# Order of VectorE's query copy and of the two folds of the exponential sums in a cached attention kernel

## The chip, the cores and the metric

One core of a Trainium2 chip. The metric is the device time of one execution in microseconds (us). The engines are named as in the profile: TensorE (PE) for matmuls, VectorE (DVE), ScalarE (ACT), GpSimd (POOL), and the queues that issue DMAs, above all SP.

## The reference

`x` has 2048 tokens of 512 values; there are 32 heads of 128, with caches of 2048 keys and values each.

```python
xn = layernorm(A_x)
q  = (xn @ A_wq) per head                       # 32 heads of 128
p  = softmax(q @ k_cache.T * 128**-0.5)         # 2048 x 2048 per head
s  = concat(p @ v_cache) @ A_wo
h  = gelu(layernorm(xn) @ B_w1)                 # then shifted by 1, -1, 2, -2 tokens
x1 = xn + shifted(h) @ B_w2
g  = silu(x1 + gelu(layernorm(x1) @ B_w3) @ B_w4)
out = A_x + s * g
```

All tensors are bf16.

## The kernel before, in words

The attention is cut into 128 **units**: groups of four heads, within each the four blocks of 512 queries, within each block the four heads. Each unit has 8 **slots**. In slot `p` of unit `u` (one turn of the loop that ends the function) TensorE makes the scores of 2 x 128 keys against 512 queries (`s_slot`, line 187): two matmuls into one of two PSUM buffers `ps_s`. ScalarE exponentiates them into `pT` (line 198). The products with the values (`pv_slot`) run some slots behind, ten in the turned units (below), so that TensorE does not wait for the exponentials. A slot thus has four matmuls, and mostly two more:

- slots 0 and 1: the queries of unit `u + 2` (`q_mm`, line 171) into the PSUM tile `ps_q`;
- slots 4 and 5: the output projection of an older block (`wo_mm`, line 291) into `ps_wo`;
- slots 2, 3, 6 and 7: a piece of the MLP branch (`ps_m`), spread over the run by a table of chunks.

`ps_q` and `ps_wo` have the same tag `xa` in the pool `psX`, which has one buffer for each tag (line 105). So the projection of slot 4 cannot start before the queries of slots 0 and 1 have been copied out by `q_copy` (line 179, VectorE, the cast at L184), and the next queries not before VectorE has added `ps_wo` to its accumulator (`wo_post`, L353).

VectorE also sums the exponentials, for the softmax's denominators. `add_first` (L204, slot 4) adds the first two `pT` tiles of a unit into `acc` (128 x 4 x 512), `add_next` (L209) adds the third in slot 6, and the fourth in slot 0 of the next unit. Then come two **folds**, of four columns to two (L214) and of two to one (L215). The function `add_last` holds the fourth add and both folds.

What remains is a sum over partitions, which is done in two ways. Outside the units 32 to 113, four matmuls against ones do it (`sums`). In the units 32 to 113 (`turned`, line 241) a DMA turns the folded `acc`: `acc_turn` (L247, issued by SP in slot 3 of the next unit) writes `accT`, and `turned_sums` reduces it on VectorE (L252) in slot 0 of the unit after. In both ways the reciprocals go to DRAM and are broadcast from there into `rb` (`bcast`, SP, L269), and `norm` multiplies the attention's result with them (L279 in turned units).

The order is written out by hand: every instruction is pinned to the program's order on its engine or queue (`pin`), and an engine takes them strictly in that order, so an instruction that waits holds up those behind it. In a turned unit VectorE's order is: reduce and reciprocal of unit `u - 2`, the fourth add and the folds of `u - 1` (slot 0), the copy of the queries (slot 2), an MLP polynomial (L454) where one is due in slot 2, `add_first` (slot 4), `wo_post` and `add_next` (slot 6), MLP work that is due then, and `norm` (slot 7). On SP: the write of the reciprocals, the broadcast (slot 2), the turn (slot 3), and then loads of keys, values and weights, which are issued well ahead of their use.

Of the kernel before, what the change touches and what calls it, by code (L numbers as in the profile page):

```python
# [17 lines left out]
def kernel(  # L18
# [32 lines left out]
    HG = 4 if H % 4 == 0 else (2 if H % 2 == 0 else 1)  # L51
# [71 lines left out]
    NU = len(units)  # L123
# [10 lines left out]
    def at(n, fn):  # L134
        todo[n].append(fn)
# [35 lines left out]
    def q_mm(u, dcs):  # L171
        g, qt, hh = units[u]
        if dcs[0] == 0:
            st[u] = dict(psq=psX.tile([P, 512], FP32, tag="xm" if u == HG else "xa", name="ps_q"))
        for dc in dcs:
            mm(st[u]["psq"][:], wqs[g * HG + hh][:, dc, :],
               xnT[:, dc, qt * 512:(qt + 1) * 512], dc == 0, dc == DC - 1)

    def q_copy(u):
        qT = qtp.tile([P, 512], BF16, name="qT")  # L180
        if u > QUIET + 1:
            pin(nc.scalar.activation(out=qT[:], in_=st[u].pop("psq")[:], func=ACT.Identity))
        else:
            pin(nc.vector.tensor_copy(out=qT[:], in_=st[u].pop("psq")[:]))  # L184
        st[u]["qT"] = qT

    def s_slot(u, p):
        g, qt, hh = units[u]
        s = st[u]
        sps = psS.tile([P, 2, 512], FP32, name="ps_s")  # L190
        for j in range(2):
            kc = 2 * p + j
            kv = kTs[g * HG + hh].rearrange("d (i p j) -> d i j p", p=P, j=KJ)
            mm(sps[:, j, :], kv[:, kc // KJ, kc % KJ, :], s["qT"][:], True, True)
        if p % 2 == 0:
            s.setdefault("pT", []).append(ptp.tile([P, 4, 512], BF16, name="pT"))
        jj = 2 * (p % 2)
        pin(nc.scalar.activation(  # L198
            out=s["pT"][-1][:, jj:jj + 2, :], in_=sps[:], func=ACT.Exp, scale=SCALE))
# [7 lines left out]
    def add_next(u, i):  # L207
        a = st[u]["acc"]
        pin(nc.vector.tensor_tensor(out=a[:], in0=a[:], in1=st[u]["pT"][i][:], op=ALU.add))  # L209

    def add_last(u):
        add_next(u, 3)
        a = st[u]["acc"]
        pin(nc.vector.tensor_tensor(out=a[:, 0:2, :], in0=a[:, 0:2, :], in1=a[:, 2:4, :], op=ALU.add))  # L214
        pin(nc.vector.tensor_tensor(out=a[:, 0, :], in0=a[:, 0, :], in1=a[:, 1, :], op=ALU.add))  # L215

    def pv_slot(u, p):
        g, qt, hh = units[u]
        s = st[u]
        if p == 0:  # L220
            s["o"] = psO.tile([P, 512], FP32, name="ps_o")
        pT = s["pT"][p // 2]
        for j in range(2):
            kc = 2 * p + j
            mm(s["o"][:], vBs[g * HG + hh][:, kc, :], pT[:, 2 * (p % 2) + j, :], kc == 0, kc == KC - 1)

    def sums(u):
        s = st[u]
        ps = psX.tile([P, 4], FP32, tag="xa" if u + 1 < QUIET else "xm", name="ps_sum")
        a = s["acc"][:, 0, :].rearrange("k (p j) -> k j p", j=4)  # L230
        for j in range(4):
            mm(ps[:, j:j + 1], a[:, j, :], ones_t[:], True, True)
        recip(s, ps)
# [7 lines left out]
    def turned(u):  # L241
        return T0 <= u < T1

    def acc_turn(u):
        s = st[u]
        s["at"] = atp.tile([P, 4, P], BF16, name="accT")
        pin(nc.sync.dma_start_transpose(out=s["at"][:], in_=s["acc"][:, 0, :]))  # L247

    def turned_sums(u):
        s = st[u]  # L250
        sm = smp.tile([P, 4], FP32, name="sm")
        pin(nc.vector.tensor_reduce(  # L252
            out=sm[:], in_=s.pop("at")[:], axis=mybir.AxisListType.X, op=ALU.add))
        recip(s, sm)
# [12 lines left out]
    def bcast(u):  # L267
        st[u]["rb"] = rp.tile([P, 512], FP32, name="rb")
        pin(nc.sync.dma_start(  # L269
            out=st[u]["rb"][:], in_=st[u]["dr"][:].rearrange("a b -> (a b)").partition_broadcast(P)))  # L270
# [20 lines left out]
    def wo_mm(g, t, hhs):  # L291
        if hhs[0] == 0:
            wo_box[0] = psX.tile([P, D], FP32, tag="xa", name="ps_wo")
        held = g == NG - 1 and (NG - 2, t // 4) in deferred
        if held and hhs[0] == 0:
            wo_part(wo_box[0][:], g - 1, t, range(HG), True, False)
        wo_part(wo_box[0][:], g, t, hhs, hhs[0] == 0 and not held, hhs[-1] == HG - 1)
# [49 lines left out]
    def wo_post(g, t):  # L347
        ps = wo_box.pop(0)
        sa = s_acc[:, t, :]
        if g == 0:  # L350
            pin(nc.vector.tensor_copy(out=sa, in_=ps[:]))
            return
        pin(nc.vector.tensor_tensor(out=sa, in0=ps[:], in1=sa, op=ALU.add))  # L353

    def wo_out(t):
        sa = s_acc[:, t, :]
        xl, gl = fin.pop(t)
        pin(nc.vector.scalar_tensor_tensor(
            out=gl[:], in0=sa, scalar=0.5, in1=gl[:], op0=ALU.mult, op1=ALU.mult))
        pin(nc.vector.tensor_tensor(out=xl[:], in0=gl[:], in1=xl[:], op=ALU.add))  # L360
        pin(nc.sync.dma_start(out=out2d[t * P:(t + 1) * P, :], in_=xl[:]))
# [361 lines left out]
    def normed(u):  # L723
        norm(u)
        gg, qq, hh = units[u]
        if hh == HG - 1 and (gg, qq) in deferred:
            pin(nc.sync.dma_start(out=o_d[qq][:], in_=oTs[(gg, qq)][:]))
        elif hh == HG - 1:
            wo_todo.extend((gg, 4 * qq + ts) for ts in range(4))
            if gg == NG - 1:  # L730
                fin_load(4 * qq)

    for n in range(NS):
        u, p = divmod(n, SPU)
        s_slot(u, p)
        lag = next(v for lim, v in LAGS if n < lim)
        while pv_done <= n - lag:
            pv_slot(*divmod(pv_done, SPU))
            pv_done += 1
        if u == 0 and p in (1, 3, 5):  # L740
            q_mm(1 + p // 2, range(DC))
        if u == 0 and p in (2, 4, 6):
            q_copy(p // 2)
        if u == HG - 2 and p in (6, 7):
            q_mm(HG, (2 * p - 12, 2 * p - 11))
        if u == HG - 2 and p == 7:
            q_copy(HG)
        if p in (0, 1) and HG - 1 <= u < NU - 2:
            q_mm(u + 2, (2 * p, 2 * p + 1))
        if p == 0 and u >= 2 and turned(u - 2):  # L750
            turned_sums(u - 2)
        if p == 0 and u >= 1:
            add_last(u - 1)
        if p == 3 and u >= 1 and turned(u - 1):
            acc_turn(u - 1)
        if p == 2 and u >= 2 and turned(u - 2):
            bcast(u - 2)
        if p == 2 and HG - 1 <= u < NU - 2:
            q_copy(u + 2)
        if p == (4 if u == T1 + 2 else 2) and u >= 2 and not turned(u - 2):  # L760
            normed(u - 2)
        if p == 3 and u >= 1 and not turned(u - 1):
            sums(u - 1)
        if p == 4 and u >= 1 and u != T1 + 1 and not turned(u - 1):
            bcast(u - 1)
        if p in (4, 5) and wo_todo:
            wo_mm(*wo_todo[0], (0, 1) if p == 4 else (2, 3))
        if p == 6 and QUIET <= u < NU - 1:
            add_next(u, 2)
        if p == 6 and wo_box:  # L770
            gg, t = wo_todo.popleft()
            wo_post(gg, t)
            if gg == NG - 1:
                at(n + 5, lambda t=t: wo_out(t))
                if t % 4 < 3:
                    fin_load(t + 1)
        if p == 4:
            add_first(u)
        if p == 4 and u == NU - 1:
            a = st[u]["acc"]  # L780
            pin(nc.vector.tensor_tensor(out=a[:, 0:2, :], in0=a[:, 0:2, :], in1=a[:, 2:4, :], op=ALU.add))
        if p == 6 and u < QUIET:
            add_next(u, 2)
        if p in (2, 3, 6, 7):
            w = 2 * u + (p >= 4)
            i = p % 2
            if i == 0:
                want = -(-(w + 1 - W0) * NCH // (W1 - W0)) if w >= W0 else 0
                window.pop("run", None)
                if done < min(want, NCH):  # L790
                    if done in hooks:
                        hooks.pop(done)(n)
                    window["run"] = chunks.popleft()
                    done += 1
            if "run" in window:
                window["run"](i, n)
        for fn in todo.pop(n, ()):
            fn()
        if p == SPU - 1 and u >= 2 and turned(u - 2):
            normed(u - 2)  # L800
        if p == SPU - 1 and u == T1 + 1:
            bcast(T1)
# [78 lines left out]
```

## Time and profile before

| | |
|---|---|
| median of 3 runs | 1278.13 us (1277.34 to 1278.28) |
| profiled execution, its time | 1277.01 us |
| its span, first to last instruction | 1275.2 us |
| mean granted TensorE clock | 0.999 |
| TensorE matmul busy | 1259.0 us |
| VectorE busy | 1094.0 us |
| ScalarE busy | 1110.9 us |
| GpSimd busy | 142.2 us |

The span runs from the first to the last instruction of one profiled execution; its time is 1.8 us longer. Busy time is the time that an engine spends in instructions. A matmul's row lasts longer than the distance to the next matmul's start, because matmuls are pipelined. In lists of groups, the columns are the source line, the engine, the operation, what is written and read, the count, and then busy us, mean ns of one, and the idle time just before them with what ended it.

### The profile page before, as it was taken

The numbers are of one execution on the slowest core, as the hardware profiler recorded it, in microseconds if no ns is written. First come the engines' busy times: TensorE is split into PE (matmuls) and PEld (weight loads), VectorE is DVE, ScalarE is ACT, GpSimd is POOL, SyncE is SP. The second block draws the span as 40 slices with busy tenths as digits, with TensorE's granted clock in tenths as the row PEclk, the third lists the DMA queues.
The fourth block names the chain that finished last, engine by engine and source line by source line (L and its number), as shares of the span: only waits on it lengthen the run. The fifth ranks groups of instructions, "written<-read, shape, count | busy, mean of one in ns | idle before, by whom it ended". The sixth has DMA issues, their size and how long they took to land.

```text
span 1275.2 us, 16720 instructions
## 1 busy us (share of the span) xinstructions
PE 1259.0 (99%) x5992; PEld 601.6 (47%) x5992; DVE 1094.0 (86%) x1489; ACT 1110.9 (87%) x1195; POOL 142.2 (11%) x241
## 2 busy tenths in 40 slices
PE   8999999999999999999999999999999999999998
PEld 5444444444444444444444444444444444444444
DVE  7888879899888988889898888988888899887886
ACT  7899998888999988899988889998888999987883
POOL 4420003334110010000000000000000000000111
PEclk9999999999999999999999999999999999999999
DMA  9644243355544454344454354535546334551532
GB/s 183 135 93 69 52 80 98 95 120 120 129 93 87 108 121 95 60 93 96 96 100 95 75 91 96 104 73 93 100 95 114 65 71 88 107 126 42 141 74 68
DMA packets 217556, 122.51 MB, mean 96 GB/s; under 512 B 169408, under 2 KB 194496, under 8 KB 217472
## 3 DMA queue, kind: packets, MB, share of 16 engines
q1 hardware_dynamic: 208512, 96.26, 38.8%
q0 software_dynamic: 8672, 24.91, 7.8%
q8 instruction: 47, 0.77, 0.3%
q14 instruction: 37, 0.30, 0.1%
q10 hardware_dynamic: 288, 0.26, 0.1%
HBM read 82.58 MB, written 7.60 MB: 71 GB/s over the span
## 4 chain that ended last, share of the span: by engine, by line
PE 69%; DVE 14%; ACT 13%; DMA 2%; issue 1%; POOL 0%; DVEq 0%; SPq 0%; POOLq 0%
PE ps_s L115 25%; PE ps_o L115 24%; ACT pT L198 9%; PE ps_m L115 7%; PE ps_wo L115 6%; PE ps_q L115 6%; DVE acc L209 4%; DVE oT L279 1%; DVE acc L214 1%; ACT pre L480 1%; DVE qT L184 1%; DVE h2T L462 1%; ACT sq L459 1%; DVE sm L252 1%; ACT sq L450 1%
## 5 line engine op out<-in xcount | busy, mean ns | idle before, releaser
L198 ACT ACTIVATE pT<-ps_s 128x1024 bf16<-128x1024 f32 x1024 | 1012.8, 1033 | 139.9 <-PE ps_s L115 130.9
L115 PE MATMUL ps_s<-qT,kT 128*128 128x512 bf16 x2048 | 608.5, 379 | 2.4 <-ACT pT L198 0.8
L115 PE MATMUL ps_o<-pT,vb 128*128 128x512 bf16 x2048 | 607.7, 379 | 0.0
L115 PEld LDWEIGHTS <-kT 128*128 128x128 bf16 x2048 | 229.4, 113 | 233.8 <-issue 21.9
L209 DVE TENSOR_TENSOR acc<-acc,pT 128x2048 bf16<-128x2048 bf16 x254 | 307.7, 1211 | 24.9 <-ACT pT L198 22.7
L115 PEld LDWEIGHTS <-vb 128*128 128x128 bf16 x2048 | 199.6, 98 | 225.3
L204 DVE TENSOR_TENSOR acc<-pT 128x2048 bf16<-128x2048 bf16 x128 | 156.2, 1220 | 28.2 <-ACT pT L198 26.7
L115 PE MATMUL ps_q<-xnT,wq_h 128*128 128x512 bf16 (+1 forms) x524 | 151.8, 374 | 2.1 <-DMA xnT<-xn 1.5
L115 PE MATMUL ps_wo<-wo_h,oT 128*128 128x512 bf16 x468 | 138.8, 379 | 2.9 <-DVE qT L184 2.6
L353 DVE TENSOR_TENSOR s_acc<-ps_wo,s_acc 128x512 f32<-128x512 f32 x100 | 68.8, 688 | 57.4 <-PE ps_wo L115 57.3
L214 DVE TENSOR_TENSOR acc<-acc 128x1024 bf16<-128x1024 bf16 x127 | 87.9, 692 | 4.3
L279 DVE TENSOR_TENSOR oT<-ps_o,rb 128x512 bf16<-128x512 f32 x82 | 87.8, 1071 | 0.1
L184 DVE CAST qT<-ps_q 128x512 bf16<-128x512 f32 x122 | 83.4, 684 | 4.8 <-PE ps_q L115 4.8
L115 PEld LDWEIGHTS <-wq_h 128*128 128x128 bf16 x524 | 50.6, 98 | 62.7 <-issue 3.1
L115 PEld LDWEIGHTS <-oT 128*128 128x128 bf16 x480 | 46.9, 98 | 63.3 <-issue 9.8
L115 PE MATMUL ps_m<-xn2T,w_sb 128*128 128x512 bf16 x224 | 66.6, 379 | 0.0
L115 PE MATMUL ps_m<-w_sb,h2T 128*128 128x512 bf16 x224 | 64.0, 379 | 0.0
L603 POOL DMA_DIRECT2D w_sb<-in_B_w_dram x28 | 21.2, 757 | 365.5 <-PE ps_m L115 330.3
L215 DVE TENSOR_TENSOR acc<-acc 128x512 bf16<-128x512 bf16 x127 | 54.0, 425 | 4.3
L252 DVE TENSOR_REDUCE sm<-accT 128x4 f32<-128x512 bf16 x82 | 55.7, 679 | 1.0 <-DMA accT<-acc 1.0
L635 POOL DMA_DIRECT2D g_d<-xr x16 | 8.8, 549 | 319.4 <-DVE xr L633 319.4
L454 DVE SCALAR_TENSOR_TENSOR sq<-sq,pre 128x1024 bf16<-128x1024 bf16 x36 | 43.8, 1217 | 0.0
(77 smaller groups left out, 613.6 us busy)
## 6 DMA issues: line engine op xcount, KB each, us to landing
rb<-dr SPq DMA_DIRECT2D x128, 256.0 KB, 4.2
vb<-in_A_v_cache_dram SPq DMA_DIRECT2D x64, 256.0 KB, 4.1
w_sb<-in_B_w_dram POOLq DMA_DIRECT2D x28, 256.0 KB, 3.9
wo_h<-in_A_wo_dram SPq DMA_DIRECT2D x32, 128.0 KB, 3.7
wq_h<-in_A_wq_dram SPq DMA_DIRECT2D x28, 128.0 KB, 3.4
kT<-in_A_k_cache_dram SPq DMA_TRANSPOSE x128, 3.8
dr<-rc SPq DMA_DIRECT2D x128, 2.0 KB, 1.4
xr<-in_A_x_dram POOLq DMA_DIRECT2D x16, 128.0 KB, 3.3
```

The source lines that it names most:

```text
L115: pin(nc.tensor.matmul(out=out, lhsT=lhsT, rhs=rhs, start=start, stop=stop))
L184: pin(nc.vector.tensor_copy(out=qT[:], in_=st[u].pop("psq")[:]))
L198: pin(nc.scalar.activation(out=s["pT"][-1][:, jj:jj + 2, :], in_=sps[:], func=ACT.Exp, scale=SCALE))
L204: pin(nc.vector.tensor_tensor(out=s["acc"][:], in0=s["pT"][0][:], in1=s["pT"][1][:], op=ALU.add))
L209: pin(nc.vector.tensor_tensor(out=a[:], in0=a[:], in1=st[u]["pT"][i][:], op=ALU.add))
L214: pin(nc.vector.tensor_tensor(out=a[:, 0:2, :], in0=a[:, 0:2, :], in1=a[:, 2:4, :], op=ALU.add))
L215: pin(nc.vector.tensor_tensor(out=a[:, 0, :], in0=a[:, 0, :], in1=a[:, 1, :], op=ALU.add))
L252: pin(nc.vector.tensor_reduce(out=sm[:], in_=s.pop("at")[:], axis=mybir.AxisListType.X, op=ALU.add))
L279: pin(nc.vector.tensor_tensor(out=oTs[(g, qt)][:, hh, :].rearrange(f, j=4), in0=s["o"].rearrange(f, j=4), in1=s["rb"].rearrange("x (p j) - ...
L353: pin(nc.vector.tensor_tensor(out=sa, in0=ps[:], in1=sa, op=ALU.add))
L454: pin(nc.vector.scalar_tensor_tensor(out=sq[:].rearrange(f2), in0=sq[:].rearrange(f2), scalar=1.0, in1=pre[:].rearrange(f2), op0=ALU.add, ...
L603: pin(nc.gpsimd.dma_start(out=w[:], in_=w3_v[:, :, fc * P:(fc + 2) * P]))
```

## The change

`add_last` is split: its add is called alone, and its two folds become `fold`. Where the sums of unit `u - 1` are not turned, the fold follows the fourth add in slot 0 as before. Where they are turned, the copy of the queries is put ahead of the folds: the fourth add in slot 0, then in slot 2 `q_copy(u + 2)` and then `fold(u - 1)`. The copy itself stays in slot 2; on VectorE nothing else stands between. On SP the broadcast of slot 2 and the turn of slot 3 keep their order.

```diff
-    def add_last(u):
-        add_next(u, 3)
+    def fold(u):
         a = st[u]["acc"]
         pin(nc.vector.tensor_tensor(out=a[:, 0:2, :], in0=a[:, 0:2, :], in1=a[:, 2:4, :], op=ALU.add))
         pin(nc.vector.tensor_tensor(out=a[:, 0, :], in0=a[:, 0, :], in1=a[:, 1, :], op=ALU.add))
...
         if p == 0 and u >= 1:
-            add_last(u - 1)
+            add_next(u - 1, 3)
+            if not turned(u - 1):
+                fold(u - 1)
+        if p == 2 and HG - 1 <= u < NU - 2:
+            q_copy(u + 2)
+        if p == 2 and u >= 1 and turned(u - 1):
+            fold(u - 1)
         if p == 3 and u >= 1 and turned(u - 1):
             acc_turn(u - 1)
         if p == 2 and u >= 2 and turned(u - 2):
             bcast(u - 2)
-        if p == 2 and HG - 1 <= u < NU - 2:
-            q_copy(u + 2)
```

## The prediction

> **What bounds the kernel now.** I read the page first: its engine totals, then its groups.
>
> ```profile
> PE 1259.0 (99%) x5992; PEld 601.6 (47%) x5992; DVE 1094.0 (86%) x1489; ACT 1110.9 (87%) x1195; POOL 142.2 (11%) x241
> ...
> L209 DVE TENSOR_TENSOR acc<-acc,pT 128x2048 bf16<-128x2048 bf16 x254 | 307.7, 1211 | 24.9 <-ACT pT L198 22.7
> ...
> L214 DVE TENSOR_TENSOR acc<-acc 128x1024 bf16<-128x1024 bf16 x127 | 87.9, 692 | 4.3
> ...
> L184 DVE CAST qT<-ps_q 128x512 bf16<-128x512 f32 x122 | 83.4, 684 | 4.8 <-PE ps_q L115 4.8
> ...
> L215 DVE TENSOR_TENSOR acc<-acc 128x512 bf16<-128x512 bf16 x127 | 54.0, 425 | 4.3
> ```
>
> TensorE is busy nearly all of the time, VectorE and ScalarE each about 87%. So an edit on VectorE can only pay where TensorE waits for VectorE. I asked for TensorE's own waits between 330 and 1140 us (the turned units). Columns: us in total, times, longest.
>
> ```profile
> PE ps_wo L115 <- DVE qT L184: 2.6, 9, 0.4
> ```
>
> That is the wait the change aims at: the output projection needs the one PSUM buffer `xa`, and the copy of the queries has not emptied it. But 2.6 us understates it. A matmul row lasts 0.379 us, while in an undisturbed stretch one starts every 0.216 us, so rows overlap by 0.163 us and a wait shows as idle only beyond that. The true loss is the distance between starts, less 0.216. The timelines of TensorE and of VectorE in unit 61 show one case (start, duration, instruction; x2 is two in a row):
>
> ```profile
> 609.44 0.59 PE L115 MATMUL ps_s<-qT,kT 128*128 128x512 bf16 x2
> 609.88 0.59 PE L115 MATMUL ps_o<-pT,vb 128*128 128x512 bf16 x2
> 610.72 0.59 PE L115 MATMUL ps_wo<-wo_h,oT 128*128 128x512 bf16 x2 [0.25 <-DVE qT L184]
> ```
>
> ```profile
> 607.69 1.20 DVE L209 TENSOR_TENSOR acc<-acc,pT 128x2048 bf16<-128x2048 bf16 x1
> 608.91 0.69 DVE L214 TENSOR_TENSOR acc<-acc 128x1024 bf16<-128x1024 bf16 x1
> 609.64 0.42 DVE L215 TENSOR_TENSOR acc<-acc 128x512 bf16<-128x512 bf16 x1
> 609.99 0.68 DVE L184 CAST qT<-ps_q 128x512 bf16<-128x512 f32 x1
> 610.59 1.22 DVE L204 TENSOR_TENSOR acc<-pT 128x2048 bf16<-128x2048 bf16 x1
> ```
>
> The last `ps_o` matmul starts at 609.88 + 0.216 = 610.09; the next should start at 610.31 and starts at 610.72, 0.05 after the copy's end: 0.42 us lost, of which the idle row shows 0.25. The queries were finished at 607.87 (last `ps_q` start 607.49 + 0.38); the copy waited only behind the two folds.
>
> Measured so over units 33 to 114, 25 of the 82 have this gap: nine of 0.42 to 0.59 us (4.09 in all; these are the nine of the wait row), three of 0.24 (0.73), thirteen of 0.12 to 0.14 (1.70). Sum **6.52 us**. In every one the projection starts about 0.05 us after the copy ends, so the copy is what ends last.
>
> The page Perfetto Trace Analysis of the Trainium skill (section Identifying the Most-Contended Engine) calls matmul busy time a poor measure of headroom, because matmuls are pipelined. The trace agrees (0.379 us rows at 0.216 us spacing): by the idle row alone the gain would be 2.6 us, by the spacing it is more.
>
> **The change, part by part.**
>
> *Nothing is added or removed:* the same instructions run, the copy moving ahead of the folds in the 82 units. Their gaps change slightly. A fold starts 0.03 after its predecessor's end, as it needs its result; the copy starts 0.08 before its predecessor's end. Putting the copy after the large add replaces a 0.03 gap by a 0.08 overlap and leaves another overlap behind it: 0.11 us of VectorE time per unit, off TensorE's path, priced at 0.
>
> *Copy earlier.* In unit 61 the copy would start near 608.81 and end at 609.49, 0.77 us before TensorE is due at 610.31. Over the 25 gaps the same sum (end of the large add - 0.08 + 0.68 + 0.05) leaves 0.59 to 1.05 us to spare. All 25 waits go: 6.52 us.
>
> *What is late next: ScalarE.* Where the exponentials run back to back, TensorE stalls shortly after anyway, at a score matmul whose PSUM buffer is not yet read. In unit 58 the projection loses 0.135 us at 581.28, and 2.7 us later the scores lose 0.085; ScalarE has no idle time between:
>
> ```profile
> 580.54 0.59 ACT L480 ACTIVATE pre<-ps_m 128x512 bf16<-128x512 f32 x1
> 581.02 1.03 ACT L198 ACTIVATE pT<-ps_s 128x1024 bf16<-128x1024 f32 x1
> 581.92 1.07 ACT L450 ACTIVATE sq<-pre 128x1024 bf16<-128x1024 bf16 x1
> 582.87 1.03 ACT L198 ACTIVATE pT<-ps_s 128x1024 bf16<-128x1024 f32 x1
> ```
>
> 0.135 + 0.085 = 0.22, and 0.22 is what a score matmul loses at the same place in units 35, 57 and 79, which have no projection gap. So that gap is paid either way. Six gaps are of this kind (units 36, 58, 80, 85, 102, 107; 0.76 us). After the other nineteen ScalarE waits for TensorE (0.58 us in unit 61) before any score stall, so the gain stands: 6.52 - 0.76 = **5.75 us**.
>
> *Folds later.* Behind them on VectorE come, in either order, the MLP's polynomial (L454) or the first add (L204); their place in the queue is unchanged. Only the turn of the sums (SP, L247) needs the second fold. In unit 61 that fold would end 0.49 us later (0.60 for the copy less 0.11), so the DMA issues 0.49 later. On SP, the key and value loads stand behind it; those are issued over a unit ahead of use. The sums are reduced (L252) in the next unit, 3.9 to 8.5 us after the issue. The DMA's rows:
>
> ```profile
> L252 DVE TENSOR_REDUCE sm<-accT x82: 667/679/693, 339.9 to 1135.8; 128x4 f32<-128x512 bf16 x82
> ...
>   DMA accT<-acc: 1.0, 2
> ...
> DMA to landing us min/median/max: 3.4/4.2/6.1
> ```
>
> Two reduces wait for it now, 1.0 us together. Pairing each issue with its landing, the others have 0.4 us or more to spare; the next two (units 114 and 110, 0.4 and 0.6) issue 2.1 and 0.9 us after the fold, since SP is still at the broadcast of the reciprocals, which hides the delay. Bounds: 0, or a loss of 1.0 (two waits of 0.49 more, wholly on the path). I take 0: the following copy has 0.6 us or more to spare, and VectorE's next idle time (0.85 us at 612.65) absorbs it.
>
> *A new wait.* The copy may now be at the queue's head before the queries are done. In 25 other units the large add ends 0.10 to 0.74 us before them; the folds filled that time, now VectorE idles: 10.6 us in all. Behind it stand the folds and L454 or L204. In unit 57 the polynomial slips from 1.29 to 1.71 us after the queries' end and would end at 2.92; ScalarE takes it up 1.56 us after its present end, in the tightest such units (60, 82, 104) 0.73 after, against a slip there of about 0.2. Then VectorE idles anyway, 0.32 and 1.17 us in unit 57 and a first idle of 0.11 or more in the others, with the larger one at the projection. Bounds: 0 to 10.6 us lost; I take 0 from those rows.
>
> **Sum.** Gain 5.75. The profiled execution has a span of 1275.2 and a time of 1277.01; it would become 1271.3. The median of the runs is 1278.13, 1.12 above it; from it I forecast **1272.4 us** (-0.45%). About 0.2%, 2.6 us, is what a measurement of this kernel can tell from no change.
>
> **Rivals.**
>
> 1. *Only part is gained.* Small shifts bring ScalarE's back-to-back stretches under more of the gaps, and only the nine long ones pay: 1278.13 - 4.09 = 1274.0, or, if only what the idle row shows, 1275.5. For it: score stalls in the turned units already lose 8.7 us. Against: ScalarE waits for TensorE between nineteen of the gaps and the next stall. Chance 0.12.
>
> 2. *The wait is elsewhere.* If the projection also waits for something that ends just after the copy, nothing moves: 1278.1. For it: the attention result it reads comes from VectorE too, so the semaphore does not name the copy. Against: the 0.05 us distance in all 25 cases, and that result is over 3 us old in unit 61. Chance 0.09.
>
> 3. *Slower: VectorE's idle time in front of the copy.* If the 10.6 us of waiting for the queries in 25 units are not absorbed, the time is 1278.13 - 5.75 + 10.64 = 1283.0. It decides where a slip of up to 0.45 us (0.74 in unit 33) exceeds the idle time behind it, or makes the polynomial late for ScalarE's tanh. For it: VectorE is 86% busy. Against: the idle rows above. Chance 0.07.
>
> The forecast has 0.72. Its own range is 1270.8 (lowest run less the whole 6.52) to 1273.5; rival 1 reaches 1275.5, so 1270.8 to 1275.6 holds 0.84. Rival 2 counts as the same, the others follow: faster 0.84, same 0.09, slower 0.07.
>
> **What would show it.** Right: no wait of `ps_wo` on `qT`; the copy directly after the third add in units 33 to 114; new idle before L184 of about 10 us, released by `ps_q`; score stalls after units 58, 80 at 0.22 where there was 0.085; reduces still waiting about 1 us in all. Wrong: projection gaps that remain though the copy is early (rival 2), ScalarE stalls that grow by more than 0.8 us (rival 1), or tanh or the reduce waiting by more than 2 us in all (rival 3).

## The result

The changed kernel takes 1272.7 us (median of 6 runs, 1272.47 to 1273.17); the kernel before, in the runs beside it, 1278.2 us. The ratio is 0.9957, 95% interval 0.9947 to 0.9967: **5.5 us faster**. The forecast was 1272.4.

### The profile page after: what moved, and what is told of

It reads as the page before. It is cut to its first block, busy times and chain, and to the rows that moved or that the text cites. A ratio compares the mean times of both kernels' runs of the same rounds, so it can differ in the third digit from the quotient of the medians.

```text
span 1270.7 us, 16602 instructions
## 1 busy us (share of the span) xinstructions
PE 1248.4 (98%) x5874; PEld 601.2 (47%) x5992; DVE 1087.2 (86%) x1489; ACT 1111.1 (87%) x1195; POOL 142.4 (11%) x241
## 4 chain that ended last, share of the span: by engine, by line
PE 74%; ACT 12%; DVE 8%; DMA 3%; issue 2%; POOL 0%; DVEq 0%; SPq 0%; ACTq 0%; POOLq 0%
PE ps_s L115 27%; PE ps_o L115 26%; ACT pT L198 9%; PE ps_m L115 8%; PE ps_q L115 7%; PE ps_wo L115 7%; DVE acc L209 3%; DMA rb<-dr 2%; ACT pre L479 1%; ACT sq L449 1%; ACT sq L458 1%; DVE oT L278 1%; DMA dr<-rc 1%; DVE qT L184 1%; DVE acc L204 1%
## 5 line engine op out<-in xcount | busy, mean ns | idle before, releaser
L115 PE MATMUL ps_o<-pT,vb 128*128 128x512 bf16 x2006 | 598.7, 379 | 3.5
L115 PE MATMUL ps_s<-qT,kT 128*128 128x512 bf16 x1991 | 596.5, 379 | 4.9 <-ACT pT L198 1.3
L184 DVE CAST qT<-ps_q 128x512 bf16<-128x512 f32 x122 | 83.7, 686 | 15.3 <-PE ps_q L115 15.2
L213 DVE TENSOR_TENSOR acc<-acc 128x1024 bf16<-128x1024 bf16 x127 | 87.0, 685 | 1.5
L214 DVE TENSOR_TENSOR acc<-acc 128x512 bf16<-128x512 bf16 x127 | 54.0, 425 | 4.4
```

The lines of the kernel that those rows point to most:

```text
L115: pin(nc.tensor.matmul(out=out, lhsT=lhsT, rhs=rhs, start=start, stop=stop))
```

## The profile after

The page of the changed kernel, by its groups (the folds are now L213 and L214):

```profile
span 1270.7 us, 16602 instructions
...
PE 1248.4 (98%) x5874; PEld 601.2 (47%) x5992; DVE 1087.2 (86%) x1489; ACT 1111.1 (87%) x1195; POOL 142.4 (11%) x241
...
L184 DVE CAST qT<-ps_q 128x512 bf16<-128x512 f32 x122 | 83.7, 686 | 15.3 <-PE ps_q L115 15.2
...
L213 DVE TENSOR_TENSOR acc<-acc 128x1024 bf16<-128x1024 bf16 x127 | 87.0, 685 | 1.5
```

TensorE's busy time cannot be compared with the 1259.0 us before: 118 matmul rows are missing from this trace (5874 of 5992), while all 5992 weight loads (PEld) are there. The idle time in front of the copy rose from 4.8 to 15.3 us, released by `ps_q`: the new wait, of the size forecast. Between 330 and 1140 us (us in total, times, longest):

```profile
DVE qT L184 <- PE ps_q L115: 9.9, 22, 0.7
```

No wait of `ps_wo` on `qT` is left in this stretch. In unit 61, TensorE and VectorE now read (start, duration, instruction):

```profile
606.96 0.59 PE L115 MATMUL ps_s<-qT,kT 128*128 128x512 bf16 x2
607.39 0.59 PE L115 MATMUL ps_o<-pT,vb 128*128 128x512 bf16 x2
607.83 0.59 PE L115 MATMUL ps_wo<-wo_h,oT 128*128 128x512 bf16 x2
```

```profile
605.23 1.19 DVE L209 TENSOR_TENSOR acc<-acc,pT 128x2048 bf16<-128x2048 bf16 x1
606.34 0.68 DVE L184 CAST qT<-ps_q 128x512 bf16<-128x512 f32 x1
606.94 0.68 DVE L213 TENSOR_TENSOR acc<-acc 128x1024 bf16<-128x1024 bf16 x1
607.65 0.42 DVE L214 TENSOR_TENSOR acc<-acc 128x512 bf16<-128x512 bf16 x1
608.00 1.22 DVE L204 TENSOR_TENSOR acc<-pT 128x2048 bf16<-128x2048 bf16 x1
```

The projection follows the `ps_o` pair after 0.44 us, two matmuls of 0.216: no gap. The copy ends at 607.02, 0.8 us before it is needed; the second fold ends at 608.07, with the projection under way; only SP waits for it.

To compare all units I measure the distance between starts, less 0.216, wherever it exceeds 0.225. A weight load starts with the matmul ahead of it (0.002 us behind it, median of the profile before), and no load is missing, so I take the distances between loads. A *gap at the projection* is such a loss in front of a `ps_wo` matmul, a *score stall* one in front of a `ps_s` matmul. Sums over units 33 to 114, in us, with the number of gaps in brackets:

| kernel | gaps at the projection | stalls at the scores | both |
|---|---|---|---|
| before | 6.52 (25) | 8.70 (88) | 15.21 |
| changed | 0 | 9.63 (90) | 9.63 |

5.58 us are gained. From the first to the last reduce of the turned units the changed kernel is 5.7 us shorter (795.82 to 790.10). The two profiled spans differ by only 4.5, since outside the turned units the same sum is 10.4 us before and 12.1 after. It lies between 10 and 12 in nine of the twelve kernels below, in old and new order alike, so it is not put down to the change; what sets it was not studied.

## The experiments

The theory: TensorE paid for the copy's lateness in 25 units and nothing else has moved. Rivals: a general shift (less VectorE time in all 82 units), or a price of the new wait or of the later turn that is hidden in the sum. Each result is a ratio to the kernel before, run beside it on the same chip, since that kernel took 1277.1 to 1277.3 us beside these runs and 1278.2 beside the changed kernel. The changed kernel was not run again, so it is compared by its ratio. The edits are shown against the changed kernel, the third against the kernel before (with `fold` as in the change); `...` stands for lines left out.

**The gap units alone.** `GAPS` holds the 25 units with a gap.

```diff
-            if not turned(u - 1):
+            if not (turned(u - 1) and u in GAPS):
                 fold(u - 1)
...
-        if p == 2 and u >= 1 and turned(u - 1):
+        if p == 2 and u >= 1 and turned(u - 1) and u in GAPS:
             fold(u - 1)
```

> The copy goes ahead of the folds only in the 25 units in which the projection started late; the other 57 turned units keep the old order. Theory (the gain is these gaps and nothing else): the whole gain, 1272.7 us, ratio to before 0.9957; no projection gap left. Rival (the gain is VectorE's 0.11 us less per unit, or a general shift of all 82 units): 25/82 of 5.5 us, so 1276.5 us.

Measured: 1271.39 us, ratio 0.9959 (0.9946 to 0.9971), the whole gain from 25 units. Projection gaps 0, score stalls 9.62.

**The other 57 alone** (`u not in GAPS` in the same two places).

> The complement: the new order only in the 57 turned units that had no gap. Theory: nothing to gain and no price, 1278.2 us within 0.2%, all 25 projection gaps still there (6.5 us between starts, if nothing shifts them), and VectorE idle about 10 us in front of the copy. Rival (a general shift): 57/82 of 5.5 us, so 1274.4 us. Second rival (the idle time in front of the copy costs): above 1279.5 us.

Measured: 1277.21 us, ratio 1.0000 (0.9990 to 1.0009). TensorE's waits and VectorE's in front of the copy, in the stretch from 330 to 1140 us:

```profile
PE ps_wo L115 <- DVE qT L184: 2.5, 9, 0.3
```

```profile
DVE qT L184 <- PE ps_q L115: 10.1, 22, 0.7
```

All gaps are there (6.35 us between starts), VectorE waits 10 us for the queries, and the time does not move: the interval allows about 1.3 us either way, and the sum of gaps and stalls is 15.1 us, before 15.2. So the general shift and a price of the new wait both fall: the 10 us are slack.

**More in front of the copy, old order.** One more add of the second fold's size, between the folds and the copy.

```diff
+    def extra(u):
+        a = st[u]["acc"]
+        pin(nc.vector.tensor_tensor(out=a[:, 1, :], in0=a[:, 2, :], in1=a[:, 3, :], op=ALU.add))
...
-            add_last(u - 1)
+            add_next(u - 1, 3)
+            fold(u - 1)
+            if turned(u - 1):
+                extra(u - 1)
```

> The old order with one more instruction of the second fold's size (128 x 512, 0.34 us from start to start) between the folds and the copy in the 82 turned units; what it writes is not used. Theory (TensorE pays for the copy's lateness one to one where there is a gap, and nothing where the copy has more spare): 19 gaps grow by 0.34 (6.5 us), six by 0.26 beyond what ScalarE costs there anyway (1.6 us), unit 38 gets one of 0.2; 1278.2 + 8.3 = 1286.5 us. Rival (VectorE's total work matters, 82 x 0.34 = 28 us at most, or not at all): above 1295 us, or 1278.2.

Measured: 1288.77 us, ratio 1.0091 (1.0078 to 1.0105), 11.6 us slower instead of 8.3. The waits, as above:

```profile
PE ps_wo L115 <- DVE qT L184: 14.6, 26, 0.9
```

The direction is as expected, and most of the places; my size was not. The extra add writes what the second fold reads, so it starts 0.03 us after that fold's end and not 0.08 before it: a step of 0.46, not 0.34. The 25 gaps grew by 0.45 to 0.50 each, and the sum over the turned units rose by 11.9 (projection 19.12, scores 7.94): one to one in these 25, once the step is right. Unit 38 got a gap of 0.74 and not of 0.2. There the fourth add itself starts later, 0.06 us ahead of the end of the queries where it was 0.48; with the unit's own 0.46 that makes 0.74 beyond a spare of 0.14. It seems that the extra add of the unit before had not been absorbed. Seven more units, which I had not named, got small gaps (0.3 us in all).

**The same work behind the folds, new order** (`extra(u - 1)` after the later `fold(u - 1)`).

> The new order with the same extra instruction behind the folds, so the same work for VectorE as in the run before, but not in front of the copy. Theory: VectorE has slack there, 1272.7 us to 1273.7 us. Rival (VectorE's total matters): as much slower against the changed kernel as the run before is against the old one, about 1281 us.

Measured: 1272.36 us, ratio 0.9961 (0.9948 to 0.9973). No projection gap, score stalls 10.13. The instruction that costs 11.6 us in front of the copy costs 0.5 us of score stalls behind it, too little to show in the time. VectorE is busy 88% of the time here and does not bound by its total; what costs is work in front of the copy.

**The copy between the folds.** `fold` gets an argument here that says which of the two it does.

```diff
             add_next(u - 1, 3)
-            if not turned(u - 1):
-                fold(u - 1)
+            fold(u - 1, (0,) if turned(u - 1) else (0, 1))
         if p == 2 and HG - 1 <= u < NU - 2:
             q_copy(u + 2)
         if p == 2 and u >= 1 and turned(u - 1):
-            fold(u - 1)
+            fold(u - 1, (1,))
```

> The copy goes between the two folds in the turned units: it is only as much earlier as the second fold is long (0.46 us with its gaps), not 1.19 us. Theory (TensorE pays for the lateness beyond its need and no more): of the 25 gaps only the two longest, units 34 and 39, keep 0.04 and 0.13 us; the same time as the changed kernel, ratio to before 0.9957. Rival (the earlier the copy, the better, in all units): 0.46/1.19 of the gain, ratio 0.9983.

Measured: 1271.77 us, ratio 0.9965 (0.9951 to 0.9978); the interval holds the changed kernel's 0.9957 and leaves out 0.9983. Unit 34 keeps 0.036 us, all other gaps are gone (39 too), and VectorE's list of waits between 330 and 1140 us has none for `ps_q`. Of the 1.19 us, 0.46 are nearly enough.

**The six gaps priced at nothing.**

```diff
+    SIX = {36, 58, 80, 85, 102, 107}
...
-            if not turned(u - 1):
+            if not (turned(u - 1) and u in SIX):
                 fold(u - 1)
...
-        if p == 2 and u >= 1 and turned(u - 1):
+        if p == 2 and u >= 1 and turned(u - 1) and u in SIX:
             fold(u - 1)
```

> The new order only in the six units 36, 58, 80, 85, 102 and 107, whose gaps of 0.12 to 0.14 us were priced at no gain because ScalarE's back-to-back stretch makes TensorE wait anyway. Theory: their projection gaps go (0.76 us), and the score stalls behind them grow from 0.08 to 0.10 to 0.22 us, so that the sum of both is the same; the time is that of the kernel before. Rival: the score stalls stay as they are and 0.76 us are gained, which the distances between starts would show.

One profiled run, 1279.63 us (too few for a ratio; it lost 3 us more outside the turned units than the kernel before). The distances decide: the six projection gaps go from 0.76 us to 0, the score stalls behind them from 0.56 to 1.31. For units 36, 58 and 80 these were 0.09, 0.08 and 0.09 and are 0.22 each. Both sums together are 15.23, before 15.21: nothing gained, as priced.

**The copy ahead of the fourth add too**: how far can VectorE wait?

```diff
-            add_next(u - 1, 3)
             if not turned(u - 1):
+                add_next(u - 1, 3)
                 fold(u - 1)
         if p == 2 and HG - 1 <= u < NU - 2:
             q_copy(u + 2)
         if p == 2 and u >= 1 and turned(u - 1):
+            add_next(u - 1, 3)
             fold(u - 1)
```

> The copy goes one step further: ahead of the fourth add as well, in all turned units, so that VectorE waits at the queue's head for the queries in most units. It tests the point from which VectorE's idle time in front of the copy costs (the rival that ended slower). In the units where the queries come late, the MLP's polynomial then starts about 2.94 us after the queries instead of 1.71 and ends at 4.16; ScalarE takes it up 0.5 us after its end in the changed kernel in eight of these units (40, 55, 60, 62, 77, 82, 99, 104), so there tanh would wait about 0.7 us. Theory: no projection gap, VectorE idle over 40 us in front of the copy, ScalarE waiting for the polynomial by some 5 us, and 3 to 6 us slower than the changed kernel: 1275.5 to 1278.5 us. Rival (VectorE's slack takes this too): 1272.7 us.

Measured: 1278.40 us, ratio 1.0009 (1.0000 to 1.0018), some 6.6 us slower than the changed kernel's ratio. Its waits, then ScalarE and VectorE at unit 60 (in brackets the idle time ahead of an instruction and what ended it):

```profile
DVE qT L184 <- PE ps_q L115: 50.6, 51, 2.9
...
ACT sq L458 <- DVE sq L453: 6.2, 10, 0.8
PE ps_s L115 <- ACT pT L198: 5.7, 17, 0.9
```

```profile
603.06 1.06 ACT L458 ACTIVATE sq<-sq 128x1024 bf16<-128x1024 bf16 x1 [0.60 <-DVE sq L453]
```

```profile
601.47 0.43 DVE L214 TENSOR_TENSOR acc<-acc 128x512 bf16<-128x512 bf16 x1
601.81 1.22 DVE L453 SCALAR_TENSOR_TENSOR sq<-sq,pre 128x1024 bf16<-128x1024 bf16 x1
```

The polynomial ends at 603.03, tanh starts at 603.06, and the exponentials and then TensorE stand behind it. The eight units named have a new score stall of 0.52 us each, unit 38 as well, unit 33 one of 0.88 more; with small ones the score stalls rise by 6.4 us, to 16.00. So the mechanism of the rival that ended slower is real. Its point lies beyond the change: there tanh came 0.53 us after the polynomial's end in these units, and here the polynomial ends 1.26 us later.

**A late turn.** Folds and turn go behind `add_first`.

```diff
-        if p == 2 and u >= 1 and turned(u - 1):
-            fold(u - 1)
-        if p == 3 and u >= 1 and turned(u - 1):
-            acc_turn(u - 1)
...
         if p == 4:
             add_first(u)
+        if p == 4 and u >= 1 and turned(u - 1):
+            fold(u - 1)
+            acc_turn(u - 1)
```

> The folds and the turn of the sums go behind the first add of the next sums, so the turn's DMA is issued 1.2 to 3.5 us later than in the changed kernel; the copy keeps its new place. It tests what a late turn costs. Theory: the reduce waits for the DMA in many units, over 10 us in all, but the copy behind it has 0.6 us or more to spare and VectorE has idle time later in the unit, so the time stays at 1272.7 to 1274 us. Rival (the way reduce, add, fold, DMA, reduce closes to a ring that is longer than a unit): 1278 us or more.

Measured: 1273.66 us, ratio 0.9979 (0.9969 to 0.9988), about 2.8 us above the changed kernel's ratio. The reduce's wait:

```profile
DVE sm L251 <- DMA accT<-acc: 11.1, 17, 1.5
```

The wait is there, over 10 us as expected, and most of it is absorbed: score stalls 9.60, no projection gap, one other stall of 0.74. The ring does not close. Where the other 2 us of the ratio come from, the one profile does not show (its own execution took 1273.17, that of the changed kernel 1272.5); that stays open.

**What is left: the score stalls.** Four edits of the changed kernel.

```diff
-        at(n + 1, square)
+        at(n + 2, square)
```

> The changed kernel with ScalarE's square of the MLP one slot later (the rest of the gelu as it is). It tests what is left: the score stalls in the turned units, 9.6 us between starts in the changed kernel, 6.9 of them in gaps over 0.1 us. Theory (they come from three extra instructions of ScalarE close together, copy, square and tanh, of which copy and square are one slot apart): most gaps of 0.22 go, and 4 to 6 us are gained if the polynomial behind the square is not made late: 1267 to 1269 us. Rival (ScalarE's total sets them): 1272.7 us.

Measured: 1279.38 us, ratio 1.0023 (1.0014 to 1.0032). My theory fell: slower by 8.4 us. In unit 60 the stalls at slots 3 and 4 were 0.22 and 0.05; now they are 0 and 0.54, and so for every pair of this kind. The score stalls of the turned units rise by 5.7 us, to 15.31; the edit also holds outside these units, where the rest was not traced to its places.

With polynomial, tanh and last product one slot later as well:

> As the run before, but square, polynomial, tanh and the last product of the gelu all go one slot later, so that the polynomial does not have to wait for the later square. Theory: the same gaps go and VectorE and ScalarE wait for nothing new, 1266 to 1268 us. Rival (the polynomial or the last product now collides with the normalisation in slot 7 or with the turn in slot 3): 1272.7 us or above.

Measured: 1280.85 us, ratio 1.0035 (1.0022 to 1.0048), score stalls 17.46. So it was not a late polynomial: in neither run does ScalarE wait for one between 330 and 1140 us.

The second idea was a backlog: an exponential takes 0.92 us from start to start, a slot with six matmuls 1.30 and one with four 0.86, so extra work of ScalarE is only absorbed in slots with six. It was put to the test with the square one slot earlier:

```diff
-        at(n + 1, square)
+        square()
```

> The changed kernel with the square of the gelu one slot earlier, directly behind the copy of the second half. The stalls that are left seem to be a backlog of ScalarE: an exponential takes 0.92 us from start to start, a slot with six matmuls 1.30 and one with four 0.86, so the extra instructions are absorbed only in slots with six, 0.38 us each; a square one slot later had one such slot less, and its stalls doubled. Theory: a square one slot earlier absorbs no more, as the slot in which it now stands would have had no idle time either; the same 0.27 us per pair, partly one slot earlier, 1272.7 us. Rival (the earlier, the better): 0.27 less per pair, some 7 us gained.

Measured: 1278.82 us, ratio 1.0014 (1.0005 to 1.0023). "No change" was wrong by 7 us. The stalls do move one slot forward (unit 60: 0.31 at slot 2, 0.05 at slot 3), but they grow by 0.09, and ten units that had none in that slot, 35 and 57 among them, get 0.31. The backlog fits the later square (one absorbing slot less, 0.27 more per pair, where such a slot absorbs up to 0.38) and the places. It does not give the size here: with the square right behind the copy the same two instructions cost more than a slot apart, and why stays open.

Last, the copy of the second MLP result on VectorE:

```diff
-                pin(nc.scalar.activation(out=pre[:, j, :], in_=mlp["ps"][:], func=ACT.Identity))
+                if j == 1 and T0 * SPU <= n < T1 * SPU:
+                    pin(nc.vector.tensor_copy(out=pre[:, j, :], in_=mlp["ps"][:]))
+                else:
+                    pin(nc.scalar.activation(out=pre[:, j, :], in_=mlp["ps"][:], func=ACT.Identity))
```

> The changed kernel with the second of each two copies of an MLP result (ps_m to pre) on VectorE instead of ScalarE in the turned units, to take 0.48 us from ScalarE's stretch. Theory: 0.38 of it was absorbed in its own slot, so each stall shrinks only by 0.1, 3 us in all, if VectorE has the 0.60 us to spare: 1269 to 1270 us. Rival (VectorE waits at its queue's head for the matmuls of that slot, and the polynomial or the normalisation behind it comes late): 1274 us or more.

Measured: 1272.72 us, ratio 0.9965 (0.9951 to 0.9978), no better than the changed kernel. Where the copy was in the way the stalls shrink by 0.11, as worked out (units 40, 55, 62: 0.22 to 0.11). But the polynomial comes late in nine units:

```profile
ACT sq L458 <- DVE sq L453: 3.4, 9, 0.6
```

These get new stalls of 0.22 to 0.53 at slot 7; the sum is 11.12 against 9.63. VectorE had the time, but not at that place. No kernel here is measurably faster than the changed one.

## Why the prediction was right, point by point

- *Loss of 6.52 us, read from starts and not from idle rows.* Right: the nine waits of the idle row and the sixteen that it does not list all went. Had 2.6 us been all there was, the time would have been 1275.5. By the page Perfetto Trace Analysis of the Trainium skill (section Identifying the Most-Contended Engine), matmul busy time misleads because matmuls are pipelined; the trace agrees in these gaps, of which the rows show 2.6 us as idle.
- *Six gaps give nothing.* Right: their score stalls grew by 0.76 us together, alone as well as in the whole change. Two more cost a little that I had not priced (units 34 and 51, 0.03 and 0.12). Gain in the turned units 5.58, forecast 5.75; the time fell by 5.5, and its interval (4.2 to 6.8) cannot tell these apart.
- *Copy early enough everywhere.* Right: with 0.46 us of the 1.19, one gap of 0.04 is left.
- *New wait of 10.6 us on VectorE, priced at 0.* Right in size (15.3 less 4.8 idle in front of the copy) and in price (the 57 units alone, ratio 1.0000). The bound of 10.6 us lost was far too wide; the rows of idle time behind it already said so.
- *Later turn, priced at 0.* Right in price: in the 57 units alone the turn comes later as well, at ratio 1.0000. The reduces' waits did not stay at about 1 us as expected but shrank: one waits now, 0.3 us in all, where two waited 1.0.
- *Rivals.* Part of the gain, and the wait elsewhere: excluded, as no projection gap is left and the 25 units alone bring the whole gain. Slower by VectorE's wait: not in this change, but shown to begin when the copy goes one instruction further ahead.

## What to carry to other kernels

When an engine runs its instructions strictly in order, ask of each what waits for it and until when, and put first the one that the bounding engine needs; the engine's share of busy time says nothing about this. Measure waits of a pipelined engine by the distance between starts, and before counting a gap as gain, look whether the next engine would make it wait a little later anyway. An instruction moved ahead of its input's arrival makes its engine wait; that is free only up to the slack of what stands behind it, which can be read from the idle times in the rows of before.

## What the runs showed of the hardware that was not expected

An instruction on VectorE that needs the result of the one ahead, or writes over what that one reads, started 0.03 us after its end; an independent one started 0.08 us before it. The first fold shows both, in all 82 turned units alike: behind the large add, as before, it starts 0.034 us after that add's end; behind the copy, as in the changed kernel, 0.081 to 0.086 us before the copy's end. So order alone changes an instruction's step by about 0.12 us: the extra 128 x 512 add took 0.46 us of the queue where 0.34 was expected.
